# A head with fewer warm-up matmuls and a new order, and attention rounds at later slots, in an attention-then-ReGLU kernel

## The chip, the cores and the metric

The kernel runs on one core of one Trainium2 chip. The metric is the device time of one execution in microseconds (us), the median over several executions. Profiles are of one execution; the span on a profile page counts from the core's first to its last instruction and is about 2 us shorter than the time of the run. The engines are TensorE (PE, matmuls; PEld is its weight load), ACT, DVE and Pool (casts, copies, exponentials, zeroing), and the DMA engines, which move data from and to memory; SP issues most of the loads. L593 is line 593 of the kernel's source.

## The reference

Block-causal attention for 8 batches of 8 heads (576 positions, head size 64), then a gated feed-forward layer on the 4608 rows of 512.

```python
scores = scale * np.matmul(q, k.transpose(0, 1, 3, 2))      # 8 x 8 x 576 x 576
scores = np.where(block_i >= block_j, scores, -1e9)         # blocks of 64
attn = softmax(scores)
x = np.matmul(attn, v)                                      # -> rows of 512
gate = np.maximum(x @ w_gate, 0.0)                          # 512 -> 1536
val = x @ w_val
out = (gate * val) @ w_out                                  # 1536 -> 512
```

## The kernel before

TensorE works through nine "tiles" of 512 rows: eight hold the first 512 positions of one batch each, the ninth all the 64-row tails. They are counted from 0: the third tile is tile 2. A tile of the feed-forward layer is 144 matmuls of 128x512, called slots here: 96 gate and value products, then 48 output products. The attention of later batches is pushed in between, at chosen slots. A "round" is the attention of one pair of heads: its scores (the visit), exponentials on ACT, zeroing of two masked corners, the two products with v (one per head), their normalisation on DVE, and the transpose into xT, which the feed-forward layer reads. The kernel's PSUM buffers are two two-bank score tiles (`sc`), one bank `one`, and three banks `ffnp` that gate, value and output products, scores and products with v all share.

The head, before the first tile, is written out by hand. `junk(n, w)` issues n matmuls of w columns whose result nobody reads. They are meant as warm-up.

```python
def junk(n, w):
    for _ in range(n):
        nc.tensor.matmul(idle[:, 0:w], ident, zeros[:, 0:w], start=True, stop=True)
...
        part(0, 0)
        junk(2, 128)
        part(0, 1)
        e0.pe_mains(1, (dve, dve), ts=(1,))
        part(0, 2)
        junk(6, 128)
        ...
        head_av(2, 1)
        to_xT_pe(1, dve)
        ...
        ffn(4)                 # four gate products
        to_xT_pe(2, act)
        both_av(3)             # fourth pair's products with v
        ffn(4)                 # first four value products
        to_xT_pe(3, dve)
```

Later slots are events: position in the tile, and what to push in there.

```python
        events = round_at(96, 4, (122, 122.1), (126, pe_xT), (6, 11))
        events += round_at(112, 5, (130, 130.1), (136, pe_xT), (4, 14))
        events += round_at(127.5, 6, (140, 141), (146, pe_xT), (4, 9))
        events += round_at(139, 7, (148, None), (153, pe_xT), (3, 7))
```

The numbers of `round_at` are: slot of the visit, round, slots of the products with v, slot of xT, and after how many slots the second exponential and the corners follow.

The softmax here doesn't subtract the row's maximum and nothing guards it: scores larger than these inputs give would overflow.

Of the kernel before, what the change touches and what calls it, by code (L numbers as in the profile page):

```python
# [17 lines left out]
def kernel(  # L18
# [319 lines left out]
    def cast_w(sts, eng):  # L338
        for dst, st in sts:
            eng(dst, st)  # L340


    def row_halves(w):
        dst, st = w
        return [(dst[:, c : c + 2], st[:, c : c + 2]) for c in (0, 2)]

    def scores(b, hp, pieces):
        sc = psum_sc.tile([128, 2, 512], FP, name="sc")
        for pos, c, main in pieces:
            for hh in range(2):  # L350
                ps = slice(64 * hh, 64 * hh + 64)
                n = 512 - 128 * c if main else 64
                o = sc[:, hh, pos : pos + n]
                if main:
                    o = o.rearrange("p (c n) -> p c n", n=128)
                nc.tensor.matmul(
                    o,
                    kTm[b % 2][ps, c, hp, :]
                    if c < 4
                    else kTt[b % 2][ps, hp : hp + 2, :].rearrange("p h n -> p (h n)"),  # L360
                    qTm[b % 2][ps, c:4, hp, :] if main else qTt[b % 2][ps, hp, :],
                    start=True,
                    stop=True,
                )
        return sc

    def part(r, i):

        pieces = [[(0, 0, True)], [(0, 1, True), (384, 3, True)], [(0, 2, True)]][i]
        sc = scores(*divmod(r, 4), pieces)  # L370
        w = (512, 512, 256)[i]
        nc.scalar.activation(
            attnT[r % 4][:, :, 512 * i : 512 * i + w], sc[:, :, 0:w], AF.Exp, scale=scale
        )
# [85 lines left out]

        return exp_last, exp_main(0), exp_main(1)

    def corners(r, zero, last=None):

        at = attnT[r % 4]
        for zero, lo, n in ((zero, 0, 512), (last or zero, 896, 128)):
            two = at[64:128, :, lo : lo + 2 * n].rearrange("p g (c n) -> p g c n", c=2)
            zero(two[:, :, :, 0:64])

# [3 lines left out]
    def normalise(out, av):  # L473
        n = av.shape[1]
        rows = av.shape[0]
        recip = sb.tile([128, NCH], FP, name="recip", bufs=4)[0:rows, 0:n]
        nc.vector.reciprocal(recip, av[:, :, 64])  # L477
        nc.vector.tensor_tensor(  # L478
            out=out,
            in0=av[:, :, 0:64],  # L480
            in1=recip.to_broadcast([rows, n, 64]),
            op=AX.mult,
        )
# [24 lines left out]
    def products_with_v(b, h, at, av):  # L508
        for p in range(4):
            for c in range(p + 1):  # L510
                col = BASE[c] + 128 * (p - c)
                nc.tensor.matmul(  # L512
                    av[:, p, :],
                    at[:, col : col + 128],
                    v_bf[b % 2][:, c, h, :],
                    start=(p == 0),
                    stop=(c == p),
                    skip_group_check=True,
                )

    def head_av(r, hh):
        b, hp = divmod(r, 4)
        h = 2 * hp + hh
        at = attnT[r % 4]
        if hh == 0:
            xnats[r] = sb.tile([128, 4, 128], BF, name="xnat", bufs=3)
        xnat = xnats[r]
        if (b > 0 or hh == 1) and (r, hh) != (4, 0):
            av = psum_ffn.tile([128, 4, 65], FP, name="ffnp")
        else:  # L530
            av = psum_one.tile([128, 4, 65], FP, name="one")
        products_with_v(b, h, at[:, hh, :], av)
        normalise(xnat[:, :, 64 * hh : 64 * hh + 64], av)

    def both_av(r):

        b, hp = divmod(r, 4)
        xnats[r] = sb.tile([128, 4, 128], BF, name="xnat", bufs=3)
        for hh in range(2):
            sc = psum_sc.tile([128, 2, 512], FP, name="sc")  # L540
            av = sc[:, 0, 0:260].rearrange("q (p e) -> q p e", e=65)
            products_with_v(b, 2 * hp + hh, attnT[r % 4][:, hh, :], av)
            normalise(xnats[r][:, :, 64 * hh : 64 * hh + 64], av)

    def xT_of(b):
        if b not in xTs:
            xTs[b] = sb.tile([128, 4, 512], BF, name="xT", bufs=3)
        return xTs[b]

    def to_xT_pe(r, evac):  # L550
        b, hp = divmod(r, 4)
        if hp >= 2:
            br = psum_one.tile([128, 1024], BF, name="one")
        else:
            br = psum_ffn.tile([128, 1024], BF, name="ffnp")
        xnat = xnats[r]
        for c in range(4):
            nc.tensor.transpose(br[:, 128 * c : 128 * c + 128], xnat[:, c, :], ident)
        evac(xT_of(b)[:, hp, :], br[:, 0:512])  # L559
# [155 lines left out]
    def ffn(n):  # L715
        for _ in range(n):
            if next(gen, 0) == 0:
                return
# [3 lines left out]
    def junk(n, w):  # L722
        for _ in range(n):
            nc.tensor.matmul(
                idle[:, 0:w], ident, zeros[:, 0:w], start=True, stop=True
            )
# [3 lines left out]
    dve, act, pool = nc.vector.tensor_copy, nc.scalar.copy, nc.gpsimd.tensor_copy  # L730
# [7 lines left out]
    with tc.manual_schedule(engines={E.PE, E.DVE, E.Activation, E.Pool, E.SP}):  # L738

        e0 = Early(0)  # L740
# [12 lines left out]
            e0.cast_qk(h0, 2, (pool, pool))  # L753
        e0.pe_mains(1, (dve, dve), ts=(0,))
        part(0, 0)
        junk(2, 128)
        part(0, 1)
        e0.pe_mains(1, (dve, dve), ts=(1,))
        part(0, 2)
        junk(6, 128)  # L760
        corners(0, zero_pool)
        e0.cast_v(0, 2, pool)
        part(1, 0)
# [1 line left out]
        part(1, 1)  # L765
        e0.pe_mains(3, (dve, dve))
        part(1, 2)
        junk(4, 128)
        corners(1, zero_dve)
        e0.cast_v(2, 2, pool)  # L770
        part(2, 0)
        junk(3, 128)
        part(2, 1)
        head_av(0, 0)
        head_av(0, 1)
# [7 lines left out]
        part(3, 1)  # L783
        head_av(2, 0)
        part(3, 2)
        head_av(2, 1)
        to_xT_pe(1, dve)
        e0.cast_v(6, 2, pool)
        (gate_01, gate_23), (val_01, val_23) = [row_halves(w) for w in w_0[0]]
        cast_w([gate_01], pool)  # L790
        corners(3, zero_pool, zero_dve)
        cast_w([gate_23], dve)
        cast_w([val_01], act)
        cast_w([val_23], pool)
        ffn(4)
        to_xT_pe(2, act)
        both_av(3)
        ffn(4)
        to_xT_pe(3, dve)
        gate_01, gate_23 = row_halves(w_0[1][0])  # L800
# [6 lines left out]
        e1, e2 = Early(1), Early(2)  # L807
# [39 lines left out]
        def round_at(p, r, av, to_xT, after=(6, 13)):  # L847

            exps = []

            def begin():
                exps.extend(visit(r))
                exps[0]()
                exps[1]()

            return [
                (p, begin),
                (p + after[0], lambda: exps[2]()),
                (min(p + after[1], av[0] - 0.5), lambda: corners(r, zero_dve)),
                *(  # L860
                    [(av[0], lambda: both_av(r))]
                    if av[1] is None
                    else [(av[i], lambda i=i: head_av(r, i)) for i in range(2)]
                ),
                (to_xT[0], lambda: to_xT[1](r)),
            ]
# [47 lines left out]
        def mains_1(hp):  # L914
# [12 lines left out]
        events = round_at(96, 4, (122, 122.1), (126, pe_xT), (6, 11))  # L927
        events += round_at(112, 5, (130, 130.1), (136, pe_xT), (4, 14))
        events += round_at(127.5, 6, (140, 141), (146, pe_xT), (4, 9))
        events += round_at(139, 7, (148, None), (153, pe_xT), (3, 7))  # L930
        events += [
            (67, lambda: cast_w(halves[1:], act)),
            (80, lambda: e1.cast_qk(0, 4, (None, dve))),
# [3 lines left out]
            (123.5, lambda: mains_1(2)),  # L937
            (132.5, lambda: mains_1(3)),
            (128, lambda: mains_2(0)),
            (142, lambda: e0.pe_tails((dve, act))),  # L940
            (143, lambda: mains_2(4)),
            (143, load_tails),
        ]
# [1 line left out]
        events = tail_at(27, 0, (40, 42)) + tail_at(43, 1, (56, 60))  # L945
        for r, p in ((8, 54), (9, 67), (10, 80), (11, 94)):
            events += round_at(p, r, (p + 21, p + 24), (p + 24, to_xT_dma))
        events += [
            (18, lambda: e1.pe_tails((dve, act))),
            *((p, lambda: late.pop(0)()) for p in (58, 70, 84, 98)),  # L950
            (45, un(2, 0, (dve, pool))),
            (48, un(2, 1, (dve, pool))),
# [9 lines left out]
        for b in range(3, B):  # L962
            events = tail_at(120, b, (136, 140))
            if b == 3:
                events += tail_at(3, 2, (21, 25))
            for i, p in enumerate((27, 50, 73, 96) if b == 3 else (2, 32, 62, 92)):
                r = 4 * b + i
                events += round_at(p, r, (p + 20, p + 24), (p + 24, to_xT_dma))
            if b + 1 < B:
                for at, which in ((9, (0, 1)), (46, (2,))):  # L970
                    events.append(
                        (
                            at,
                            lambda b=b, w=which: load_qkv(
                                b + 1, w, products[-1] if w == (0, 1) else None
                            ),
                        )
                    )
                events.append((66, lambda b=b: dma_transposes(b + 1)))
            run(144 * (b - 1), events)  # L980
# [30 lines left out]
```

## Time and profile before

| | before |
|---|---|
| time, median | 364.5 us |
| span of the profile | 362.5 us |
| TensorE busy | 354.9 us, 98% |
| first value product | 19.31 us |

The first lines of the page of the kernel before: engine, busy us, share of the span, instructions.

```profile
span 362.5 us, 7493 instructions
PE 354.9 (98%) x2978; PEld 176.6 (49%) x2978; DVE 168.3 (46%) x395; ACT 169.3 (47%) x280; POOL 111.9 (31%) x146
```

A busy share of 98% does not say that every microsecond is work: a 128x512 matmul is shown as 0.38 us long, though the next one can start 0.216 us after it (four take 0.86 us, from 112.28 to 113.14 us before), so waits up to 0.16 us stay hidden. So I take a wait as the distance between the starts of two successive matmuls less what the first usually takes: 0.216 us for 128x512, 0.22 for four transposes, 0.30 for ten products of 65 columns.

The head is where TensorE does not set the pace. The chain of waits of the kernel before, in order of time (start us, us, what):

```profile
11.39 7.22 DMA stage<-in_moe_w_val_dram
18.64 0.63 ACT wv L340
19.31 0.60 PE ffnp L593 x2
```

And the timeline of the same stretch (start us, us, engine, line, operation, tile written <- read; in brackets the engine's idle time and what ended it):

```profile
15.61 0.61 POOL L340 CAST wg<-stage 128x512 bf16<-128x512 f32 x1 [0.61 <-DMA stage<-in_moe_w_gate_dram]
17.08 0.81 PE L593 MATMUL ffnp<-xT,wg 128*128 128x512 bf16 x3 [0.41 <-DVE xT L559]
18.64 0.62 ACT L340 CAST wv<-stage 128x512 bf16<-128x512 f32 x1 [2.10 <-DMA stage<-in_moe_w_val_dram]
19.31 0.60 PE L593 MATMUL ffnp<-xT,wv 128*128 128x512 bf16 x2 [0.59 <-ACT wv L340]
```

The gate weights are there at 15.6 us. The value weights are there 3.0 us later, and the first value product has to wait for them. The 0.5 MB loads that follow are cast on Pool every 1.5 us (20.15, 21.65, 23.16 us).

### The profile page before, as it was taken

The numbers are of one execution on the slowest core, as the hardware profiler recorded it, in microseconds if no ns is written. First come the engines' busy times: TensorE is split into PE (matmuls) and PEld (weight loads), VectorE is DVE, ScalarE is ACT, GpSimd is POOL, SyncE is SP. The second block draws the span as 40 slices with busy tenths as digits, with TensorE's granted clock in tenths as the row PEclk, the third lists the DMA queues.
The fourth block names the chain that finished last, engine by engine and source line by source line (L and its number), as shares of the span: only waits on it lengthen the run. The fifth ranks groups of instructions, "written<-read, shape, count | busy, mean of one in ns | idle before, by whom it ended". The sixth has DMA issues, their size and how long they took to land.

```text
span 362.5 us, 7493 instructions
## 1 busy us (share of the span) xinstructions
PE 354.9 (98%) x2978; PEld 176.6 (49%) x2978; DVE 168.3 (46%) x395; ACT 169.3 (47%) x280; POOL 111.9 (31%) x146
## 2 busy tenths in 40 slices
PE   7999999999999999999999999999999999999996
PEld 3544454545554455444544455445544454444443
DVE  4843565555534543545444434543455434333432
ACT  5853566587047543653266624564355333302310
POOL 6556647499039000850067003900000000000000
PEclk9999999999999999999999999999999999999999
DMA  8999999999999952997389964999100220021014
GB/s 254 287 356 373 305 224 286 172 161 176 155 235 141 144 134 80 99 137 167 102 59 138 159 132 53 145 129 155 64 17 14 74 81 0 2 87 29 2 37 108
DMA packets 150387, 49.58 MB, mean 137 GB/s; under 512 B 132816, under 2 KB 143312, under 8 KB 150352
## 3 DMA queue, kind: packets, MB, share of 16 engines
q0 software_dynamic: 70320, 8.85, 48.7%
q1 hardware_dynamic: 74944, 31.47, 40.6%
q10 hardware_dynamic: 5088, 8.78, 7.5%
q8 instruction: 23, 0.38, 0.5%
q14 instruction: 12, 0.10, 0.1%
HBM read 37.75 MB, written 9.44 MB: 130 GB/s over the span
## 4 chain that ended last, share of the span: by engine, by line
PE 92%; DMA 3%; SPq 2%; DVE 1%; issue 0%; ACT 0%
PE ffnp L593 50%; PE ffnp L678 25%; PE ffnp L512 5%; PE sc L399 3%; PE ffnp L492 3%; DMA stage<-in_moe_w_val_dram 2%; SPq L139 2%; PE one L399 2%; PE one L593 1%; DMA stage<-in_k_dram 1%; PE sc L433 1%; PE sc L593 1%; DVE xnat L478 0%; PE one L433 0%; PE sc L239 0%
## 5 line engine op out<-in xcount | busy, mean ns | idle before, releaser
L609 DVE TENSOR_TENSOR hT<-gate_sb,ffnp 128x512 bf16<-128x512 bf16 x106 | 72.6, 686 | 98.0 <-PE ffnp L593 72.1
L603 ACT ACTIVATE gate_sb<-ffnp 128x512 bf16<-128x512 f32 x103 | 61.8, 602 | 90.0 <-PE ffnp L593 90.0
L678 PE MATMUL ffnp<-wo,hT 128*128 128x512 bf16 (+2 forms) x444 | 101.5, 373 | 0.0
L593 PE MATMUL ffnp<-xT,wv 128*128 128x512 bf16 x376 | 99.9, 379 | 0.6 <-ACT wv L340 0.6
L593 PE MATMUL ffnp<-xT,wg 128*128 128x512 bf16 x364 | 98.8, 379 | 0.5 <-DVE xT L559 0.4
L593 PEld LDWEIGHTS <-wg 128*128 128x128 bf16 x432 | 40.1, 98 | 45.9 <-issue 3.6
L593 PEld LDWEIGHTS <-wv 128*128 128x128 bf16 x432 | 39.9, 98 | 46.0 <-issue 2.3
L678 PEld LDWEIGHTS <-hT 128*128 128x128 bf16 x444 | 40.6, 98 | 42.3 <-issue 1.1
L408 ACT ACTIVATE attnT<-sc 128x1024 bf16<-128x1024 f32 x56 | 56.9, 1041 | 0.0
L282 POOL DMA_DIRECT2D q_bf<-in_q_dram x20 | 17.7, 903 | 93.2 <-DVE hT L609 79.5
L688 DVE COPY ob<-ffnp 128x512 f32<-128x512 f32 (+2 forms) x37 | 25.0, 676 | 40.4 <-PE ffnp L678 40.1
L512 PEld LDWEIGHTS <-attnT 128*128 128x128 bf16 x640 | 26.0, 98 | 14.6 <-DVE xnat L478 3.8
L477 DVE RECIPROCAL recip<-ffnp 128x4 f32<-128x4 f32 (+1 forms) x72 | 12.9, 179 | 32.6 <-PE ffnp L512 23.1
L512 PE MATMUL ffnp<-v_bf,attnT 128*128 128x65 bf16 x560 | 26.1, 194 | 0.0
L414 ACT ACTIVATE attnT<-one 128x256 bf16<-128x256 f32 x28 | 10.7, 384 | 32.4 <-PE ffnp L399 30.0
L478 DVE TENSOR_TENSOR xnat<-ffnp,recip 128x256 bf16<-128x256 f32 x56 | 23.7, 424 | 2.2 <-DVE recip L477 0.3
L282 POOL DMA_DIRECT2D v_bf<-in_v_dram x25 | 21.4, 934 | 0.9 <-DMA k_bf<-in_k_dram 0.9
L454 ACT ACTIVATE attnTt<-one 64x256 bf16<-64x256 f32 x8 | 3.0, 377 | 36.5 <-PE ffnp L433 36.5
L282 POOL DMA_DIRECT2D k_bf<-in_k_dram x20 | 17.8, 942 | 0.0
L399 PE MATMUL sc<-qTm,kTm 64*128 64x512 bf16 (+1 forms) x168 | 17.1, 305 | 0.0
L399 PEld LDWEIGHTS <-kTm 64*128 64x128 bf16 x224 | 9.3, 94 | 15.6 <-issue 10.9
L445 ACT ACTIVATE attnTt<-sc 128x1024 bf16<-128x1024 f32 x16 | 15.7, 1016 | 0.0
(98 smaller groups left out, 253.0 us busy)
## 6 DMA issues: line engine op xcount, KB each, us to landing
out_dram<-ob ACTq DMA_DIRECT2D x29, 256.0 KB, 2.5
stage<-in_moe_w_gate_dram SPq DMA_DIRECT2D x6, 512.0 KB, 9.0
stage<-in_moe_w_val_dram SPq DMA_DIRECT2D x6, 512.0 KB, 8.8
stage<-in_moe_w_out_dram SPq DMA_DIRECT2D x6, 512.0 KB, 10.5
q_bf<-in_q_dram POOLq DMA_DIRECT2D x20, 128.0 KB, 4.2
k_bf<-in_k_dram POOLq DMA_DIRECT2D x20, 128.0 KB, 5.2
v_bf<-in_v_dram POOLq DMA_DIRECT2D x20, 128.0 KB, 6.2
stage<-in_v_dram SPq DMA_DIRECT2D x19, 128.0 KB, 5.0
```

The source lines that it names most:

```text
L282: ins = nc.gpsimd.dma_start(dst, src[b, :, 128 * c : 128 * c + n, :].rearrange("h p d -> p h d"),)
L399: nc.tensor.matmul(where[c].rearrange("p (c n) -> p c n", n=128), kTm[b % 2][head_of(hh), c, hp, :], qTm[b % 2][head_of(hh), c:4, hp, :], ...
L408: return lambda: nc.scalar.activation(at[:, :, lo : lo + 512], sc, AF.Exp, scale=scale)
L445: return lambda: nc.scalar.activation(at[:, :, 2 * i : 2 * i + 2, 0:256], main[i].rearrange("p g (h n) -> p g h n", h=2), AF.Exp, scale=scale,
L477: nc.vector.reciprocal(recip, av[:, :, 64])
L478: nc.vector.tensor_tensor(out=out, in0=av[:, :, 0:64], in1=recip.to_broadcast([rows, n, 64]), op=AX.mult,)
L512: nc.tensor.matmul(av[:, p, :], at[:, col : col + 128], v_bf[b % 2][:, c, h, :], start=(p == 0), stop=(c == p), skip_group_check=True,)
L593: nc.tensor.matmul(to, (wg, wv)[t][f // 4][:, c, 128 * (f % 4) : 128 * (f % 4) + 128], x[:, c], start=(c == 0), stop=(c == 3),)
L603: nc.scalar.activation(gate_sb, gate, AF.Relu)
L609: nc.vector.tensor_tensor(out=h, in0=gate_sb, in1=val, op=AX.mult)
L678: nc.tensor.matmul(op, hT[f][:, 128 * s : 128 * (s + 1)], wo[f // 4][:, f % 4, n0:n1], start=(f == 0), stop=(f == 11),)
L688: nc.vector.tensor_copy(ob, op)
```

## The change

The intent: shorten the head by taking out warm-up matmuls and letting each engine work on what is needed next; move work out of the busy end of tile 0; give batch 3's rounds, in the third tile, more room. The diff, cut to its core:

```diff
-        junk(2, 128)                       # after part(0, 0)
-        junk(6, 128)
+        junk(1, 512)
-        junk(4, 128)
+        junk(1, 256)
-        junk(3, 128)                       # after part(2, 0)
...
+        to_xT_pe(1, dve)
+        corners(3, zero_dve, ((896, 128),))
         head_av(2, 1)
-        to_xT_pe(1, dve)
-        corners(3, zero_pool, zero_dve)
-        cast_w([gate_23], dve)
+        corners(3, zero_pool, ((0, 512),))
+        cast_w([gate_23], pool)
         ffn(4)
+        both_av(3)
         to_xT_pe(2, act)
-        both_av(3)
         ffn(4)
...
-        events += round_at(139, 7, (148, None), (153, pe_xT), (3, 7))
+        events += round_at(140.5, 7, (150.5, None), (155, pe_xT), (3, 8))
-            (142, lambda: e0.pe_tails((dve, act))),        # tile 0
-            (18, lambda: e1.pe_tails((dve, act))),         # tile 1
+            (16, lambda: e0.pe_tails((dve, act))),
+            (20, lambda: e1.pe_tails((dve, act))),
...
-            for i, p in enumerate((27, 50, 73, 96) if b == 3 else (2, 32, 62, 92)):
+            for i, p in enumerate((27, 51, 75, 99) if b == 3 else (2, 32, 62, 92)):
-                events += round_at(p, r, (p + 20, p + 24), (p + 24, to_xT_dma))
+                av = (p + 19, p + 21) if b == 3 else (p + 20, p + 24)
+                events += round_at(p, r, av, (av[1], to_xT_dma))
```

More of the change, by code (lines that the diff above doesn't have):

```diff
@@ L461, in tail_visit, with corners @@
         return exp_last, exp_main(0), exp_main(1)
-    def corners(r, zero, last=None):
+    def corners(r, zero, which=((0, 512), (896, 128))):
         at = attnT[r % 4]
-        for zero, lo, n in ((zero, 0, 512), (last or zero, 896, 128)):
+        for lo, n in which:
             two = at[64:128, :, lo : lo + 2 * n].rearrange("p g (c n) -> p g c n", c=2)
```

## The prediction

> **What bounds the kernel now.** TensorE. The page gives PE 354.9 of 362.5 us busy, and the chain of waits is 92% PE. From the starts of successive matmuls in the timeline, a 128x512 product costs 0.216 us, and from 19.3 us to the end there are few holes. The head is different. In the waits, the first value product at 19.31 us waits for ACT's cast of the value weights (18.64 us), and that cast waits for a DMA: the chain shows "DMA stage<-in_moe_w_val_dram", issued 11.39, 7.22 us. Before that the exponentials fill ACT without a hole (12 in 9.86 us, from 6.68 to 16.54 us).
>
> **What changes.**
>
> 1. Head. Fifteen 128-column warm-up matmuls become 768 columns (one of 512, one of 256). Gate products no longer wait 0.58 us at 17.08 for the second pair's xT, and both products with v come before the third pair's transposes. All this lies before 19.31 us, where the DMA decides; no DMA issue before it moves. The PE only waits longer for the same landing. Expected gain 0.0 us (-0.2 to +0.3). [...] the trace shows the cold rate as 0.427 us per 512 columns until 4.2 us and 0.216 us later. [...] So no cost.
>
> 2. Boundary of tiles 0 and 1 (55 to 64 us). Batch 0's tail transposes (0.32 us for eight, plus a 0.16 us wait) leave tile 0 and return in tile 1: work moved, not saved. Round 7's visit one slot later removes a 0.24 us wait for ACT's copy of kT. But the visit now follows a product with v, and its second score tile takes the PSUM buffer that ACT frees last (copy of xT, until 55.4 us): about 0.2 us, and the score pairs then lose their overlap (0.1 us each, as at 115 us). Products with v two slots later leave nothing between them and the value product that takes their buffer: this wait grows from 0.16 to about 0.6 us. xT two slots later leaves one product (0.22 us) to cover a copy that takes 0.68 us from the transposes' end: a new wait of about 0.45 us at the first products of c=3. Net loss about 0.5 us (0 to 0.9).
>
> 3. Third tile (101 to 140 us). Here visits at 115.24 and 121.72 us wait 0.40 and 0.15 us for a PSUM buffer (releaser DVE xnat), and each then loses 0.31 us because the row pairs no longer overlap (normally 0.09). At 129.07 another 0.16 us. Together about 1.16 us. With products with v at +19 and +21 and visits at +24 the buffer is free in time; a new wait of about 0.15 us at the following gate product may appear, three times. Net gain about 0.8 us (0.4 to 1.1).
>
> **Sum.** 0.0 - 0.5 + 0.8: about 0.4 us faster on 364.5, thus 364.1 us, 363.2 to 364.8. Chances: faster by over 2% 0.005, within 2% 0.99, slower by over 2% 0.005.
>
> **What would show it.** Head: first value product still at 19.3 us behind the same DMA. Boundary: waits at the value product after round 7's products with v and at c=3. Third tile: no "one then ffnp" gap in the two visits; the tile 0.8 us shorter. Tiles from the fourth on unchanged (38.6 us each).
>
> **What would make it wrong.** The value weights landing at another time (then the head counts one for one); [...] the boundary's waits hidden because DVE and ACT run ahead.

Two passages on TensorE's clock are cut out of this text, where marked, because no trace or run here showed what they said: the reason for "So no cost" in step 1, and one of the things that would make the forecast wrong. No term of the sum is cut: it stands at 0.0 - 0.5 + 0.8, which adds to 0.3 and was recorded as about 0.4 us faster; the clock is in it at no cost.

## The result, and the profile after

| | before | after |
|---|---|---|
| time, median (range) of 4 runs each | 364.46 us (364.25 to 364.54) | 364.73 us (364.47 to 364.77) |
| ratio after/before | | 1.0007, 95% interval 0.9989 to 1.0024 |

A ratio is the mean time of one kernel's fast runs over that of the other's of the same rounds, so not quite the ratio of the medians. The two kernels are equal within what was measured. The predicted 364.1 us (363.2 to 364.8) holds, though the predicted gain of 0.4 us did not appear. The traces show that two of the three steps behind it did not happen as told, and the errors cancelled.

The page of the kernel after:

```profile
span 362.9 us, 7464 instructions
PE 355.3 (98%) x2965; PEld 176.1 (49%) x2965; DVE 168.2 (46%) x394; ACT 168.8 (47%) x280; POOL 112.3 (31%) x147
```

To see where the time went I use the weight loads of the feed-forward products. The traces hold all 1308 of them for every kernel here (some matmul records are missing), so the n-th of one kernel can be set beside the n-th of another. I worked out this table from their starts, in us (a weight load can start a little ahead of its matmul, 17.90 against 17.96 us at the first value product after):

| stretch | before | after | after less before |
|---|---|---|---|
| to the first value product (5th) | 19.31 | 17.90 | -1.41 |
| to the first output product of tile 0 (97th) | 21.94 | 22.12 | +0.18 |
| to four before the end of tile 0 (141st) | 14.85 | 15.70 | +0.85 |
| through the boundary and tile 1 (289th) | 44.54 | 45.28 | +0.74 |
| through the third tile and 16 products of the fourth (449th) | 45.49 | 45.50 | +0.01 |
| to the 1296th | 211.59 | 211.61 | +0.02 |

These are single executions. Nine profiles of this document have the head of the kernel after, word for word; in the eight of them whose loads did not stall, the first value product starts at 17.96 to 18.29 us. Three have the same tile 0 as well (after, after_old_third_tile, after_av_18_21), and their stretch from the 97th to the 141st is 15.70, 15.90 and 15.34 us. So a few tenths in the head or in that stretch need no cause in the code. In the same three, the stretch through the boundary and tile 1 differs by only 0.03 us.

Below, "third tile" stands for the stretch from the 289th to the 449th.

**The head became 1.4 us faster.** The timeline of the kernel after, same stretch:

```profile
15.58 0.62 POOL L340 CAST wg<-stage 128x512 bf16<-128x512 f32 x1 [0.56 <-DMA stage<-in_moe_w_gate_dram]
16.25 1.04 PE L593 MATMUL ffnp<-xT,wg 128*128 128x512 bf16 x4
17.05 0.62 ACT L340 CAST wv<-stage 128x512 bf16<-128x512 f32 x1 [0.60 <-DMA stage<-in_moe_w_val_dram]
17.96 0.59 PE L593 MATMUL ffnp<-xT,wv 128*128 128x512 bf16 x2
```

The gate products run without the hole at 17.08 us, as intended. But the product at 17.96 us became possible because the value weights came 1.6 us earlier, though their load was issued at the same moment (11.39 us before, 11.40 after).

**Most of it was given back between 40 and 48 us.** The chain of waits of the kernel after no longer goes from the value weights into TensorE. It stays with the loads until 47 us (DMA, Pool's cast of v, and the products with v that read it):

```profile
40.40 5.57 DMA stage<-in_v_dram
46.11 1.06 POOL v_bf L181
47.22 0.47 PE one L512 x10
```

**The boundary of tiles 0 and 1 lost 0.74 us.** TensorE's timeline of the kernel before, from round 7's products with v (L512) on:

```profile
59.08 0.78 PE L512 MATMUL sc<-v_bf,attnT 128*128 128x65 bf16 x20
59.70 0.60 PE L593 MATMUL ffnp<-xT,wv 128*128 128x512 bf16 x2
60.29 0.60 PE L593 MATMUL sc<-xT,wv 128*128 128x512 bf16 x2
...
61.60 0.38 PE L593 MATMUL sc<-xT,wv 128*128 128x512 bf16 x1
61.85 0.59 PE L593 MATMUL ffnp<-xT,wg 128*128 128x512 bf16 x2
```

The same of the kernel after:

```profile
58.43 0.77 PE L512 MATMUL sc<-v_bf,attnT 128*128 128x65 bf16 x20
59.63 0.61 PE L593 MATMUL sc<-xT,wv 128*128 128x512 bf16 x2 [0.43 <-DVE xnat L478]
...
60.95 0.38 PE L593 MATMUL sc<-xT,wv 128*128 128x512 bf16 x1
61.62 0.59 PE L593 MATMUL ffnp<-xT,wg 128*128 128x512 bf16 x2 [0.30 <-DVE xT L559]
```

Twenty products take 0.62 us (59.08 to 59.70 before). After, the next product starts 1.20 us after the first of the twenty (58.43 to 59.63): a wait of 0.58 us. It writes the score tile that the first product with v has just used and DVE is still reading (xnat, L478, 59.15 to 59.57 us). Before, two value products lay between. The second wait is 61.62 - 60.95 - 0.216 = 0.45 us: the first product of the fourth quarter of x waits for DVE's copy of xT (L559, 61.15 to 61.57 us).

**The third tile is unchanged.** Before, the second score product of a visit waits (114.84 to 115.24 us, 0.40 us):

```profile
114.84 0.28 PE L399 MATMUL one<-qTm,kTm 64*128 64x256 bf16 x1
115.24 0.28 PE L399 MATMUL ffnp<-qTm,kTm 64*128 64x256 bf16 x1
...
115.89 0.39 PE L593 MATMUL ffnp<-xT,wg 128*128 128x512 bf16 x1
```

After, the visit is clean (both at 115.97 and 115.98 us), but the gate product behind the second product with v starts 0.47 us after it instead of 0.30:

```profile
114.75 0.47 PE L512 MATMUL ffnp<-v_bf,attnT 128*128 128x65 bf16 x10
115.22 0.82 PE L593 MATMUL ffnp<-xT,wg 128*128 128x512 bf16 x3
115.97 0.28 PE L399 MATMUL one<-qTm,kTm 64*128 64x256 bf16 x1
115.98 0.28 PE L399 MATMUL ffnp<-qTm,kTm 64*128 64x256 bf16 x1
```

Three waits went (0.40, 0.15, 0.16 us) and three of 0.17 us came, with 0.05 us ahead of each first product with v: 0.71 against 0.66 us.

### The profile page after: what moved, and what is told of

Same layout as the page of the kernel before. It is cut to its first block, busy times and chain, and to the rows that moved or that the text cites. A ratio compares the mean times of both kernels' runs of the same rounds, so it can differ in the third digit from the quotient of the medians.

```text
span 362.9 us, 7464 instructions
## 1 busy us (share of the span) xinstructions
PE 355.3 (98%) x2965; PEld 176.1 (49%) x2965; DVE 168.2 (46%) x394; ACT 168.8 (47%) x280; POOL 112.3 (31%) x147
## 4 chain that ended last, share of the span: by engine, by line
PE 85%; DMA 9%; SPq 2%; POOL 1%; DVE 0%; issue 0%; ACT 0%; POOLq 0%; ACTq 0%
PE ffnp L593 46%; PE ffnp L678 24%; PE ffnp L512 5%; DMA stage<-in_k_dram 4%; PE sc L399 3%; DMA stage<-in_moe_w_val_dram 3%; PE ffnp L492 3%; DMA stage<-in_v_dram 3%; SPq L139 2%; PE one L399 2%; PE sc L433 1%; POOL v_bf L181 0%; PE one L433 0%; PE one L593 0%; PE ffnp L260 0%
## 5 line engine op out<-in xcount | busy, mean ns | idle before, releaser
L512 PEld LDWEIGHTS <-attnT 128*128 128x128 bf16 x640 | 25.9, 98 | 15.6 <-DVE xnat L478 3.8
L512 PE MATMUL ffnp<-v_bf,attnT 128*128 128x65 bf16 x560 | 26.1, 194 | 0.0
L478 DVE TENSOR_TENSOR xnat<-ffnp,recip 128x256 bf16<-128x256 f32 x56 | 23.8, 425 | 1.9
```

The source lines that it names most:

```text
L478: nc.vector.tensor_tensor(out=out, in0=av[:, :, 0:64], in1=recip.to_broadcast([rows, n, 64]), op=AX.mult,)
L512: nc.tensor.matmul(av[:, p, :], at[:, col : col + 128], v_bf[b % 2][:, c, h, :], start=(p == 0), stop=(c == p), skip_group_check=True,)
```

## The experiments

Twelve kernels ran, all correct within the tolerance of the comparison. "Before" ran again: 364.41, 364.38, 364.28 and 364.35 us. A few runs of before, and some of three variants, were 1 to 4 us longer; I read medians. Except for the last kernel, the intervals of the ratios are wider than, or as wide as, the differences of some tenths discussed here (0.9910 to 1.0028 for after_one_load_less), so the argument rests on the stretches of the traces, and the times only agree with it.

### Why did the value weights land earlier?

The packets of the loads give a hint. In every trace one packet of 16 KB in a queue of kind "instruction" appears near that time. The queues in the window from 16.2 to 16.6 us of the kernel before (packets, MB, share of 16 engines):

```profile
q1 hardware_dynamic: 141, 0.14, 105.9%
q8 instruction: 1, 0.02, 17.5%
```

and in the window from 17.0 to 17.4 us of the kernel after (its window from 16.2 to 16.6 us has no such line):

```profile
q1 hardware_dynamic: 136, 0.14, 107.8%
q8 instruction: 1, 0.02, 17.7%
```

It starts at 16.39 us before and at 17.17 us after, and takes 1.12 and 1.13 us; a load packet of 1 KB takes 0.05 us there. I counted the load packets in flight from their starts and durations: 17.5 on average in a full microsecond before it, 16.4 while it runs, 17.5 after, in both kernels. So this packet seems to take one of the 16 engines away from the loads for 1.1 us; the trace does not name the engine. How one packet could make a whole load late is not shown either. In thirteen of the fourteen profiles one of the two loads that land next after this packet is 0.6 to 1.5 us later than the pace of 1.5 us: the value weights before, the second half of the gate weights after (cast at 20.00 us, 2.95 us behind the value weights). In the fourteenth, after_old_boundary, whose loads had stalled earlier, none is.

This does not settle the mechanism. Up to 1.5 us late is more than the packet's 1.1 us, and the next packet of this kind (27.95 us before, 1.10 us long; 29.43 us after, 1.08 us) is followed by no late load in either kernel: the casts behind it stay 1.34 to 1.38 us apart. Why the first is and the second is not, is not shown.

Theory A: the packet fetches TensorE's instructions, and its moment depends on how many TensorE has consumed. This was my conjecture, and "fetch" below is its word for the packet. The name of the queue's kind fits, and so does the count: from the first to the last of the 23 packets of the kernel before, TensorE starts 2740 weight loads, 124.5 a packet, each with a matmul; DVE, ACT and Pool together have only 821 counted instructions. And when the second packet starts, TensorE has started 224 to 231 weight loads in all fourteen profiles, though the time runs from 23.54 to 30.63 us. (At the first it is 144 to 167, so that one is not tied to one count.) Rival B: the new order of casts and products does it. Rival C: TensorE's lighter load in the head does it.

**junk_only**: the kernel before, with only the warm-up matmuls changed.

```diff
-        junk(2, 128)
-        junk(6, 128)
+        junk(1, 512)
-        junk(4, 128)
+        junk(1, 256)
-        junk(3, 128)
```

> The kernel before with only the change of the warm-up matmuls (15 of 128 columns become one of 512 and one of 256). Theory A (instruction count): an instruction fetch of 16 KB, which occupies one DMA engine for 1.1 us, starts at 16.4 us before and delays the value weights from about 17.0 to 18.6 us; with 13 fewer matmuls it starts about 17.2 us, behind the value weights. Then ACT's first cast of the value weights starts near 17.0 us here too (before 18.64, after 17.05), though the order of the head is the old one, and the first value product starts between 18.4 and 18.7 us, since both products with v still end there. Rival B (order): the new order of casts and products lets the transfer land earlier; then the cast stays at 18.6 us and the product at 19.3 us. Total: A about 0.3 us under before, because waits for the output weights and for v near 42 to 47 us take the rest back; B equal to before.

Measured: 364.19 us; fetch at 17.19 us, value cast at 16.93 us, first value product at 18.56 us:

```profile
16.93 0.62 ACT L340 CAST wv<-stage 128x512 bf16<-128x512 f32 x1 [0.38 <-DMA stage<-in_moe_w_val_dram]
18.56 0.60 PE L593 MATMUL ffnp<-xT,wv 128*128 128x512 bf16 x2
```

The old order with the new warm-up has the early weights. Rival B falls. The order is worth the rest of the head, 0.6 us (18.56 against 17.96 us; 0.3 to 0.6 us with the spread of the head given above), once the weights are there. The time was 0.2 us under before, where 0.3 us was expected.

**junk_same_columns**: the kernel before, with the same 1920 warm-up columns in five matmuls.

```diff
-        junk(2, 128)
+        junk(1, 256)
-        junk(6, 128)
+        junk(1, 512)
+        junk(1, 256)
-        junk(4, 128)
+        junk(1, 512)
-        junk(3, 128)
+        junk(1, 384)
```

> The kernel before with the same number of warm-up columns (1920) in five matmuls in place of fifteen: TensorE's load in the head is the same, its instructions are 20 fewer. Theory A (count of TensorE's instructions decides when the fetch comes): the fetch moves to about 17 us, the value weights are cast near 17.0 us. Rival C (less TensorE work in the head, whatever the count): cast stays at 18.6 us.

Measured: 364.19 us; fetch at 16.86 us, value cast at 17.10 us. TensorE's columns are those of the kernel before; only its instructions are 20 fewer (ten matmuls, each with a weight load). Rival C falls.

**after_count_back** and **after_count_more**: the kernel after with matmuls of 32 columns put back in the same four places, 13 and 36 of them.

```diff
+        junk(2, 32)     # after part(0, 0);   8 in after_count_more
         junk(1, 512)
+        junk(5, 32)     #                    10
         junk(1, 256)
+        junk(3, 32)     #                    10
+        junk(3, 32)     # after part(2, 0);   8
```

> The kernel after with thirteen matmuls of 32 columns put back where the warm-up matmuls were, 26 TensorE instructions with hardly any work; the new order stays. Theory A: the fetch comes again before the value weights have landed, the cast of the value weights starts near 18.6 us and the first value product near 19.3 us. Rival B: 17.0 and 17.9 us as in the kernel after. Total: A about 0.3 us over the kernel after (365.0), B equal to it (364.7).

> The kernel after with 36 matmuls of 32 columns in the places of the removed warm-up matmuls, 72 TensorE instructions. The run with 26 put back gave a fetch at 16.46 us, at the edge: its profiled execution still had the value weights at 17.25 us, its others were slower. Theory A: with 72 the fetch comes before 16.2 us; the gate or the value weights are then about 1.1 to 1.5 us late (gate cast after 16.5 or first value cast after 18.0 us), while the share of busy DMA engines falls by one of sixteen for 1.1 us from the fetch on. Rival B (the order of casts and products brings the gain): first value cast stays near 17.0 us.

Measured: after_count_back 365.26 us (364.84 to 365.65), fetch at 16.46 us, but in the profiled run, its fastest, the value cast is at 17.25 us. Here the expectation failed in the trace: the fetch starts 0.8 us before the value weights land, as it says, but they are on time, and the next load (gate weights, cast at 20.11 us) is the late one. after_count_more 365.55 us, fetch at 15.81 us, and the value weights are late again, with the new order of the head:

```profile
18.39 0.62 ACT L340 CAST wv<-stage 128x512 bf16<-128x512 f32 x1 [1.74 <-DMA stage<-in_moe_w_val_dram]
19.07 0.60 PE L593 MATMUL ffnp<-xT,wv 128*128 128x512 bf16 x2 [0.85 <-ACT wv L340]
```

The head of before beside those of the five kernels that change it:

| kernel | TensorE instructions in the head, against before | fetch starts | first value cast |
|---|---|---|---|
| after_count_more | +46 | 15.81 us | 18.39 us |
| before | 0 | 16.39 us | 18.64 us |
| after_count_back | 0 | 16.46 us | 17.25 us |
| junk_same_columns | -20 | 16.86 us | 17.10 us |
| junk_only | -26 | 17.19 us | 16.93 us |
| after | -26 | 17.17 us | 17.05 us |

So far theory A stands: the instruction count orders the fetches (of the other eight profiles with the head of the kernel after, seven have the first at 17.13 to 17.76 us, and the one whose loads stalled at 18.39 us), and the second fetch moves with it too (27.95 us before, 29.43 after, 23.54 in after_count_more). The value weights are late in the two profiles whose fetch starts by 16.39 us, and on time in those where it starts from 16.46 us on, the stalled one aside. That fewer TensorE instructions bring the value weights earlier is shown by junk_only and junk_same_columns (cast at 16.93 and 17.10 us, 18.64 before); that it is the packet's hold on one DMA engine that does it fits (16.4 load packets in flight against 17.5), but is inferred. That the edge lies there, and that the slower runs of after_count_back are executions on the wrong side of it, is argued from one profile each, not shown.

### Where did the head's gain go?

**after_one_load_less**: the kernel after without one 0.5 MB load that stands in the stream ahead of the output weights. The cast of k for four heads of batch 1 reads the q stage instead. This is wrong, though the comparison's tolerance let it pass.

```diff
-                self.st[0, h0], self.st[1, h0] = new_stage(1024), new_stage(1024)
+                self.st[0, h0] = self.st[1, h0] = new_stage(1024)
+                if self.b == 2:
+                    self.st[1, h0] = new_stage(1024)
...
-            self.load(self.st[1, h0], k, h0, n, k_eng)
+            if (self.b, n) != (1, 4):
+                self.load(self.st[1, h0], k, h0, n, k_eng)
```

> The kernel after without the load of batch 1's k for heads 0 to 3 (0.5 MB); its cast reads the q stage instead, so the result is wrong on purpose. Theory: the head's gain of 1.2 us is lost between 42 and 47 us to three waits (0.26, 0.20, 0.35 us) for output weights and v, because the stream of loads is full from 11 to 46 us and gained nothing. With 0.5 MB less, about 1.4 us of the stream, these waits go and the gain of the head is kept: the 124th to 140th output product 0.8 us earlier than in the kernel after (slot 140 at 54.9 us, not 55.7), total 363.9 to 364.1 us. Rival: TensorE, ACT or Pool sets the pace there; then slot 140 stays at 55.7 us and the total at 364.7 us.

Measured: 364.20 us, just over the expected 363.9 to 364.1; the 141st weight load at 54.90 us as expected (55.73 after); the stretch from the 97th to the 141st takes 14.82 us, as before (14.85). TensorE of the kernel after around the products with v of round 4:

```profile
44.50 2.53 PE L678 MATMUL ffnp<-wo,hT 128*128 128x512 bf16 x10
47.22 0.47 PE L512 MATMUL one<-v_bf,attnT 128*128 128x65 bf16 x10 [0.19 <-POOL v_bf L181]
```

and with one load less (its lines are numbered three higher):

```profile
44.29 2.33 PE L681 MATMUL ffnp<-wo,hT 128*128 128x512 bf16 x10
46.46 0.47 PE L515 MATMUL one<-v_bf,attnT 128*128 128x65 bf16 x10
```

Ten output products take 2.16 us. With one load less the products with v follow 2.17 us after their start, without a wait. In the kernel after they follow after 2.72 us: 0.20 us of that is a wait for output weights, 0.35 us the wait for v. A third wait, 0.26 us, lies at 42.46 us. So the loads set the pace from 42 to 47 us in the kernel after. The change only moved a delay from one load to the next, it hardly shortened the stream: v of batch 1 is cast 0.28 us earlier than in the kernel before, where TensorE comes later (its ten output products start at 45.47 us) and its products with v follow after 2.16 us, without a wait. Pool before, then after:

```profile
46.39 1.05 POOL L181 CAST v_bf<-stage 128x1024 bf16<-128x1024 f32 x1 [0.98 <-DMA stage<-in_v_dram]
46.11 1.05 POOL L181 CAST v_bf<-stage 128x1024 bf16<-128x1024 f32 x1 [1.02 <-DMA stage<-in_v_dram]
```

A head that is 1.4 us ahead therefore arrives 0.34 us ahead at slot 124 (48.57 against 48.91 us).

### Was the boundary the loss?

**after_old_boundary**: the kernel after with round 7 and the tail transposes in their old places.

```diff
-        events += round_at(140.5, 7, (150.5, None), (155, pe_xT), (3, 8))
+        events += round_at(139, 7, (148, None), (153, pe_xT), (3, 7))
+            (142, lambda: e0.pe_tails((dve, act))),        # tile 0
-            (16, lambda: e0.pe_tails((dve, act))),         # tile 1
-            (20, lambda: e1.pe_tails((dve, act))),
+            (18, lambda: e1.pe_tails((dve, act))),
```

> The kernel after with round 7 and batch 0's tail transposes where they were before. Theory: the waits of 0.59 us (value product after round 7's products with v), 0.46 us (first product of c=3) and 0.17 us (tail transposes) go, those of before (0.24, 0.16, 0.11, 0.16 us) return; about 0.6 us faster than the kernel after, 364.1 us, and 0.3 us under the kernel before. Rival: the boundary is in step with DMA or Pool and only the place of the wait changes; then equal to the kernel after within 0.15 us.

Measured: 364.23 us (363.78 to 364.69), 0.5 us under the kernel after; the stretch through the boundary and tile 1 takes 44.55 us (45.28 after, 44.54 before). The change there cost 0.73 us. The profiled execution was the slowest of the four: between 10 and 14 us fewer of its loads were in flight (13 to 21 in most samples and 2 at 10.8 us, against 17 to 26 before), the gate weights were cast only at 17.16 us (15.58 after), and the value weights came one load later, at 18.6 us. Its fetch starts only at 18.39 us, just before they land. Its head is no evidence for or against theory A. Why the loads stalled is open.

### Was the third tile a gain?

**after_old_third_tile**: the kernel after with batch 3's rounds in their old places.

```diff
-            for i, p in enumerate((27, 51, 75, 99) if b == 3 else (2, 32, 62, 92)):
+            for i, p in enumerate((27, 50, 73, 96) if b == 3 else (2, 32, 62, 92)):
-                av = (p + 19, p + 21) if b == 3 else (p + 20, p + 24)
-                events += round_at(p, r, av, (av[1], to_xT_dma))
+                events += round_at(p, r, (p + 20, p + 24), (p + 24, to_xT_dma))
```

> The kernel after with the old places of batch 3's rounds in the third tile. The prediction's step 3 says 0.8 us slower than after (365.5). The two traces say: three waits of 0.41, 0.14 and 0.16 us return, three of 0.17 us and small ones of 0.05 us go, so equal within 0.1 us (364.7), and the third tile (first gate weights of tile 2 to first of tile 3) takes 45.5 us as in both kernels.

Measured: 364.82 us (364.28 to 365.04), equal to the kernel after. The third tile takes 45.25 us, even 0.25 us less than with the new places: the wait that was 0.40 us in the kernel before is 0.16 us here. What made the difference between the two was not followed up. That the total is equal all the same comes from tile 0, which has the same code in both (15.90 us against 15.70 from the 97th to the 141st).

**after_av_18_21**: the kernel after with the first product with v one slot earlier.

```diff
-                av = (p + 19, p + 21) if b == 3 else (p + 20, p + 24)
+                av = (p + 18, p + 21) if b == 3 else (p + 20, p + 24)
```

> The kernel after with batch 3's products with v at +18 and +21 in place of +19 and +21. Reading of the trace: the gate product after the second product with v takes the PSUM buffer of the first and waits 0.17 us for DVE to normalise it, because only two gate or value products (0.43 us) and one product with v (0.30 us) lie between. With three products between (0.65 + 0.30 us) the wait should go, three times: 0.4 to 0.5 us less in the third tile than after, 364.3 us in all. Rival: another buffer or DVE becomes the wait, less than 0.15 us gained.

Measured: 364.93 us, third tile 45.61 us. The rival was right:

```profile
113.44 0.38 PE L593 MATMUL ffnp<-xT,wv 128*128 128x512 bf16 x1
113.93 0.48 PE L512 MATMUL ffnp<-v_bf,attnT 128*128 128x65 bf16 x10
...
114.89 0.47 PE L512 MATMUL ffnp<-v_bf,attnT 128*128 128x65 bf16 x10
115.20 0.81 PE L593 MATMUL ffnp<-xT,wg 128*128 128x512 bf16 x3
```

The last distance is now 0.31 us, so the wait at the gate product is gone. But the first product with v starts 0.49 us after one value product, a wait of 0.27 us. TensorE waits there for DVE's zeroing of the corners (memset of attnT, L733, 113.70 to 114.00 us), which stands on DVE behind a product of gate and value that waits for ACT.

### Four attempts at a better kernel

All four keep the head of the kernel after.

**best_old_third**: a mended boundary, round 4 two slots later, the old third tile.

```diff
-        events = round_at(96, 4, (122, 122.1), (126, pe_xT), (6, 11))
+        events = round_at(96, 4, (124, 124.1), (128, pe_xT), (6, 11))
-        events += round_at(127.5, 6, (140, 141), (146, pe_xT), (4, 9))
-        events += round_at(140.5, 7, (150.5, None), (155, pe_xT), (3, 8))
+        events += round_at(127.5, 6, (140.5, 141), (146, pe_xT), (4, 9))
+        events += round_at(140, 7, (148, None), (153, pe_xT), (3, 3.5))
-            (16, lambda: e0.pe_tails((dve, act))),
-            (20, lambda: e1.pe_tails((dve, act))),
+            (17, lambda: e0.pe_tails((dve, act))),
+            (21, lambda: e1.pe_tails((dve, act))),
```

> The kernel after with its head, the third tile of before, and a mended boundary: round 7's visit at 140 ahead of round 6's products with v, round 7's products with v back at 148 and xT at 153, its corners zeroed ahead of the last output copy of the tile, the tail transposes at 17 and 21 of tile 1; and round 4's products with v two slots later (124), so that two output products cover their wait for v. Theory: of the boundary's 1.2 us of new waits about 1.0 goes (0.59, 0.46 and 0.17 us become about 0.2 together), of the 0.35 us wait for v nearly all; together 363.6 us (363.3 to 364.0), 0.7 to 0.8 us under the kernel before. Rival: the waits turn up at the next product that needs the same buffer or copy; 364.2 us or more.

**best_20_25** and **best_18_21_corners**: the same, but with batch 3's visits at 27, 51, 75 and 99 and

```diff
+                av = (p + 20, p + 25) if b == 3 else (p + 20, p + 24)    # best_20_25
+                av = (p + 18, p + 21) if b == 3 else (p + 20, p + 24)    # best_18_21_corners
+                events += round_at(
+                    p, r, av, (av[1], to_xT_dma), (6, 12) if b == 3 else (6, 13)
+                )
```

> As best_old_third, but batch 3's rounds at 27, 51, 75, 99 with products with v at +20 and +25. The second score tile of a visit then takes the buffer of the first product with v after three products, not two or zero, and no gate product takes a buffer just used. Expected: no wait over 0.1 us at the three visits, the third tile 0.3 to 0.5 us shorter than with the old places, 363.2 us. Rival: the second product with v waits for DVE in its place, no gain.

> As best_old_third, but batch 3's rounds at 27, 51, 75, 99 with products with v at +18 and +21, and the zeroing of their corners one slot earlier (+12), ahead of a product of gate and value on DVE. In the run with +18 and +21 alone the first product with v waited 0.27 us for that zeroing, which stood behind a DVE product that waited for ACT. Expected: both the 0.27 and the 0.17 us waits gone, third tile 0.3 to 0.5 us shorter than with the old places, 363.2 us. Rival: DVE's order only moves the wait, no gain.

Measured, with the stretches of the table above:

| | time | 97th to 141st | boundary and tile 1 | third tile |
|---|---|---|---|---|
| after | 364.73 us | 15.70 | 45.28 | 45.50 |
| best_old_third | 364.81 us | 16.69 | 44.54 | 45.24 |
| best_20_25 | 365.53 us | 16.58 | 44.48 | 45.55 |
| best_18_21_corners | 364.32 us | 16.57 | 44.48 | 44.82 |

All three missed their times by about 1.1 to 2.3 us. The boundary did as expected. The third tile did with +18 and +21 and the earlier corners (0.7 us less than after); with +20 and +25 the next gate product waits 0.39 us for ACT instead. The loss is round 4's new place. TensorE of best_18_21_corners:

```profile
47.63 0.40 PE L239 MATMUL sc<-ident,q_bf 128*128 128x128 bf16 x4 [0.54 <-POOL q_bf L168]
48.19 0.40 PE L239 MATMUL sc<-ident,k_bf 128*128 128x128 bf16 x4 [0.16 <-POOL k_bf L168]
...
48.63 0.47 PE L512 MATMUL one<-v_bf,attnT 128*128 128x65 bf16 x10
```

The products with v no longer wait for v, but now transposes come ahead of them that wait for q and k, which Pool casts after v. The shift covered one wait and uncovered the next of the same chain of loads and casts.

**best_no_av4**: as best_18_21_corners, with round 4 back at 122.

```diff
-        events = round_at(96, 4, (124, 124.1), (128, pe_xT), (6, 11))
+        events = round_at(96, 4, (122, 122.1), (126, pe_xT), (6, 11))
```

> As best_18_21_corners, with round 4's products with v back at 122. There the move to 124 put the transposes of batch 1's third pair ahead of them, which wait for Pool's cast of q (0.70 and 0.33 us) and then for ACT (0.65 us): the last output products of tile 0 came 0.9 us later than in the kernel after. Theory: these waits go, the mended boundary (0.8 us against after) and third tile (0.7 us) stay; slot 140 near 55.7 us, and 363.3 us in all (363.0 to 363.7), 1.0 us under the kernel before. Rival: the waits at the boundary return because round 7 now runs ahead of its data; 364.0 us or more.

Measured: 363.01 us (362.90 to 363.11, six runs), at the low end of what was expected, against 364.35 us for before on the same chip; ratio 0.9953, interval 0.9932 to 0.9973. All six runs lie below the lowest of the twelve of before (363.89 us). It beats both kernels: by 1.3 us the kernel before, by 1.7 us the kernel after (medians, the latter from another batch). Its page:

```profile
span 361.3 us, 7417 instructions
PE 351.3 (97%) x2916; PEld 175.7 (49%) x2965; DVE 168.4 (47%) x394; ACT 168.8 (47%) x280; POOL 112.1 (31%) x147
```

Its stretches are 18.19, 22.04, 15.36, 44.48, 44.82 and 211.6 us. Less those of the kernel after, the 97th to 141st saves 0.34, the boundary 0.80, the third tile 0.68 us; the head is 0.29 us later. The 0.34 and the 0.29 us are within the spread of unchanged code given above; the boundary and the third tile are the change's own. (PE's smaller busy time is partly missing records: 2916 matmuls of the 2965 that its weight loads show.)

## Why the prediction was right or wrong

- **The total** was right: 364.1 us with 363.2 to 364.8, measured 364.73, and "within 2%". It was right by cancellation, and its sum, 0.0 - 0.5 + 0.8 ("about 0.4 us faster"), did not happen: by the traces the kernel gained 0.4 us up to the 141st weight load, lost 0.74 us at the boundary and gained nothing in the third tile. That the total still fell into the range is luck.
- **Step 1, the head: wrong.** The step that failed is "no DMA issue before it moves. The PE only waits longer for the same landing." No issue moved (11.39 and 11.40 us), and the landing did, by 1.6 us: with fewer TensorE instructions the value weights land early (junk_only and junk_same_columns show it), most likely since the instruction packet moved behind them (17.19 and 16.86 us, 16.39 before). The prediction named "the value weights landing at another time" as what could make it wrong, but also said the head would then "count one for one". It did not: of 1.41 us, 0.34 was left at slot 124, as the loads set the pace again from 42 us on.
- **The clock:** "no cost" was right. In the trace after, matmuls of 512 columns are 0.43 us apart and take 0.63 us each up to 4.17 us; from 6.27 us on they take 0.37 to 0.39 us. No slow ones came back. TensorE is never idle for 0.5 us between there and 22 us, so this trace does not say what a longer idle stretch does to that pace. (The page's row of the granted clock shows a 9, 90% or more, in all 40 slices, the first with the slow matmuls too, so it says nothing on this.)
- **Step 2, the boundary: mechanism right, size a little small.** The waits at the value product (0.58 us, predicted 0.6), at c=3, the first products of the fourth quarter of x (0.45, predicted 0.45), and at the visit (0.21, predicted 0.2) came where they were named; the one at the visit lies ahead of the 141st weight load, in place of one of 0.24 us that went. A wait of 0.17 us of the tail transposes for ACT was not. The loss was 0.74 us, predicted 0.5 in a range of 0 to 0.9.
- **Step 3, the third tile: wrong in size.** The step is "each then loses 0.31 us because the row pairs no longer overlap". That was no loss. From the second score product to the next gate product before takes 0.65 us (115.24 to 115.89) after the wait and as much (108.81 to 109.46) in a clean visit. I summed the lengthened distances and not the shortened ones between them. The real waits were 0.71 us, not 1.16. The new waits were sized right (0.17 us, three times), and 0.05 us ahead of each first product with v was missed. Predicted gain 0.8 us, measured 0.0.

## What to carry to other kernels

A wait for a load says when it landed, not why so late: if loads of one size land at an even pace except one, look at what else the DMA engines carried then, packets of kind instruction among it (here one of 16 KB for 1.12 us; that it was the cause is inferred). Time won upstream of a full stream of loads came back here as waits at later loads (1.41 us became 0.34), so follow the gain through by stretches, for instance by the n-th weight load, before you count it. When you shift an event by a slot, write down for every shared buffer and every queue which release now lies in front of it; several waits here were set by how much work lay between a buffer's last reader and its next writer (0.58 us at the boundary, three of 0.17 us in the third tile). And before you explain a few tenths, look how far executions of unchanged code differ in that stretch.
